# A decode step of attention and GLU layers: transposes of a kept V tile moved, one weight load halved, one sum read from PSUM

## The chip, the cores and the metric

The kernel runs on one core of one Trainium2 chip. The metric is the device time of one execution in microseconds (us). Before the change the median of three runs is 180.24 us (179.0 to 181.01).

## What is computed

Four rows of activations (batch 4, one position each, width 512) pass through attention, a gated linear unit (GLU), and then both again with the same weights and caches. There are 32 query heads on 8 key/value heads, and a window of the last 2048 positions.

```python
def _A_ref(x, k_cache, v_cache, wq, wo):
    ...
    q = (lambda x, *d: x.transpose(*d))((x @ wq).reshape(B, Sq, Hq, Dh), 0, 2, 1, 3)
    k = jnp.repeat(k_cache[:, :, Sk - W:, :], rep, axis=1)
    v = jnp.repeat(v_cache[:, :, Sk - W:, :], rep, axis=1)
    scores = jnp.einsum("bhqd,bhkd->bhqk", q, k) * (Dh ** -0.5)
    p = _softmax(scores, axis=-1)
    o = jnp.einsum("bhqk,bhkd->bhqd", p, v)
    return (lambda x, *d: x.transpose(*d))(o, 0, 2, 1, 3).reshape(B, Sq, Hq * Dh) @ wo

def _B_ref(x, w_gate, w_up, w_down):
    ...
    h = _sigmoid(g) * u
    return jnp.einsum("bsf,fd->bsd", h, w_down)

x = A_x
x = x + _A_ref(_layernorm(x, axis=-1), A_k_cache, A_v_cache, A_wq, A_wo)
x = x + _B_ref(_layernorm(x, axis=-1), B_w_gate, B_w_up, B_w_down)
x = x + _A_ref(_layernorm(x, axis=-1), A_k_cache, A_v_cache, A_wq, A_wo)
x = x + _B_ref(_layernorm(x, axis=-1), B_w_gate, B_w_up, B_w_down)
```

Both passes use the same weights and caches; `B_x` is not used.

## The kernel before

**A plan, then an order.** The Python code first records operations (`P.op`) with the tokens that they read and write and the PSUM banks that they touch. A list scheduler with assumed durations then gives each engine its order, and semaphore waits are derived from the dependencies. From the second attention on, the TensorE operations keep the order in which they were recorded (`P.chain`). An extra edge (`after=`, or `deps.add`) forces an order that the data alone do not ask for.

**Loads.** SyncE issues all weight and cache loads from line 398, in one fixed order, on one queue. SBUF is an arena of 50 slots of 512 KB (128 partitions by 4 KB). K of all eight heads stays resident for the second attention, as do the output weights `wo`. V tiles (1 MB each, one for a head `h` and a pair of batch rows `bp`) are mostly loaded again. Around the first GLU, where K and `wo` hold nearly all slots, pieces of 448 or 512 KB pass through a few half slots: `GB` (a pair), `GA` (V of head 6), and `Y` and `Z` (the two V tiles of head 7). The gate pieces go, in order, to GB0, GB1, GA0 and Y0; the up pieces to Y1, Z0, GB0 and GB1; then come the down pieces and the second attention's query weights. A load is issued as soon as the readers of its half slot are done.

**V kept in PSUM.** So that the tile `Y` and half of `Z` need not be read from HBM again, their contents are parked in PSUM banks: VectorE transposes them there in 128x512 fp32 blocks. `stash` (line 574) does four blocks of `Y`, called st0 to st3; st0 and st1 free the half Y0, st2 and st3 the half Y1. `stash_half` (line 596) does two blocks of `Z`, called so0 and so1. Later transposes bring them back (lines 589 and 602).

**The end of the first attention.** For each head, `pv_unit` multiplies V by the probabilities (line 966), VectorE normalises (`oe`, line 974), TensorE regroups the heads (`pm`, line 984) and VectorE masks the outcome (`oq`, line 989). `wo_unit` (line 1153) then multiplies by the head's output weights, accumulating in PSUM bank WB; x itself was added into the same bank at the start. After the eighth head `attn_add(0)` (line 1278) sums the four head groups in WB to the new x.

**Layer norm and GLU.** `layer_norm` sums x over its four column groups (`ln_red`, line 740), a matmul with ones gives the mean (line 743), and two subtractions (lines 746 and 750) give the centred x, as bf16 for the matmuls (`xn`) and in fp32. The GLU's gate and up products follow (line 1330, one piece of weights after the other), the gate's exponential, and the down product (line 1396). The second layer norm then feeds the query products (line 788). In the last GLU the down product runs at line 1371; its four blocks of 128 columns are copied from PSUM by ScalarE and VectorE in turn (`oc0` to `oc3`, line 1382) and one DMA writes the output.

Of the kernel before, what the change touches and what calls it, by code (L numbers as in the profile page):

```python
# [9 lines left out]
ALU = mybir.AluOpType  # L10
AXX = mybir.AxisListType.X
# [267 lines left out]
def build(nc, A_x, A_k, A_v, A_wq, A_wo, B_wg, B_wu, B_wd, out, cfg=None):  # L279
    cfg = dict(cfg or {})  # L280
    tm = dict(_TM)
# [40 lines left out]
    with es:  # L322
# [57 lines left out]
        def slot_ap(s):  # L380
            return arena[:, s * SLOT:(s + 1) * SLOT]

        def tile_ap(s):
            return arena[:, s * SLOT:(s + 2) * SLOT]
# [4 lines left out]
        def c_dve(n, rate=None):  # L389
            return tm["dve_fix"] + n * (tm["dve_f32"] if rate is None else rate)  # L390
# [147 lines left out]
        def load_wo(hh):  # L538
            left["wo", hh] = 4

            def emit(s):
                for n in range(2):
                    dma("wo%d" % (2 * hh + n), slot_ap(s + n), wo_d[:, 2 * hh + n, :], w=[("slot", s + n)], rate="bw_4k")

            if 2 * hh + 2 < HKV:
                load(("wo", hh), 4, "bw_4k", (2 * SLOT, wo_d[:, hh * 2:(hh + 1) * 2, :], False))
            else:
                loads.append((("wo", hh), emit))
# [31 lines left out]
        def named(name):  # L580
            return [o for o in P.ops if o.name == name]
# [9 lines left out]
                    o.deps.update(fresh)  # L591
            loads.append((name, emit))

        def stash_half(n, name):
            src = slot_ap(base[Z])[:, n * 1024:(n + 1) * 1024].bitcast(F32)
            P.op("vector", "so%d" % n, c_dve(512), lambda v: v.transpose(ps[:, OBS[n], :], src),
                 r=[("slot", base[Z])], w=[("so", n)], banks=(OBS[n],), after=[o for o in P.ops if o.name == name])

        def unstash_half(after):
            for n in range(2):  # L600
# [126 lines left out]
        def bview(t, b0, b1):  # L727
            return t.rearrange("p (c b) -> p c b", b=NB)[:, :, b0:b1]

        def layer_norm(tag, b0, b1, for_q):  # L730
            ds = tm["dve_small"]
            nb = b1 - b0
            xts = [("xT", b) for b in range(b0, b1)]
# [2 lines left out]
            msq = ps[:, CB, 200:200 + nb]  # L736
            ones_d = inv_d[:, 0:1].broadcast_to([128, 128])
            x2 = xT[:, NX:2 * NX]
            P.op("vector", "ln_red" + tag, ds,
                 lambda v: v.tensor_reduce(lnr[:, 0:nb], xT[:, 0:NX].rearrange("p (c b) -> p b c", c=NC), AXX, ALU.add),  # L740
                 r=xts, w=[("lnr", 0)])
            P.op("tensor", "ln_sum" + tag, tm["pe_f32"],
                 lambda t: t.matmul(mean, ones_d, lnr[:, 0:nb], start=True, stop=True),
                 r=[("lnr", 0), ("inv_d",)], w=[("cb",)], banks=(CB,))
# [399 lines left out]
        def wo_unit(tag, h, ov, k2, first, final):  # L1144
            name = ("wo", h // 2)
            s = need(name)
            o = h % 2 * REP * D

            def e_wo(pe):
                last = None  # L1150
                for r_ in range(REP):
                    for c in range(NC):
                        last = pe.matmul(ps[:, WB, c * NR:(c + 1) * NR],  # L1153
                                         tile_ap(s)[:, o + r_ * D + c * 128:o + r_ * D + (c + 1) * 128],
                                         ov[:, r_ * NR:(r_ + 1) * NR], start=(first and r_ == 0 and c == 0),
                                         stop=(final and r_ == REP - 1), skip_group_check=True)
                return last
            P.op("tensor", "WO%s_%d" % (tag, h), NC * REP * tm["pe_pair"], e_wo,
                 r=[("slot", s + h % 2)] + [("op", k2)], w=[("psw",)], banks=(WB,))
            done(name)  # L1160

        def attn_first():
            def front(h):
                k_transpose(h)
                softmax_unit("0.%d" % h, h)
                turn = lambda: turn_p(0, "0.%d" % h, h % 2, PBS[h % 2])
                return turn

            for h in range(2):
                front(h)()  # L1170
            for h in range(HKV):
                tag = "0.%d" % h
                turn = front(h + 2) if h + 2 < HKV else None
                if h == HKV - 1:
                    stash(stashed, (0, 1, 2))
                    need(Z)
                op = pv_unit(tag, h, h % 2, v_tiles[(0, h)])
                if h == HKV - 1:
                    st = stash(stashed, (3,), named("oe" + tag))
                    named("oq" + tag)[0].deps.add(st)  # L1180
                    stash_half(0, "oq" + tag)
                if turn is not None:
                    turn()
                wo_unit(tag, h, op, h % 2, False, h == HKV - 1)

        def attn_second():
            hs = list(range(HKV))[::-1]
# [99 lines left out]
                 lambda v: v.tensor_tensor(xT[:, 0:NX], xT[:, NX:2 * NX], xT[:, 0:NX], ALU.add),  # L1287
                 r=[("x2",)] + [("xT", b) for b in range(NB)], w=[("xT", b) for b in range(NB)])

        def glu(k, b0, b1, last=False):  # L1290
            nb = b1 - b0
            variance = layer_norm("G%d" % k, b0, b1, False)
            if k == 0:
                stash_half(1, "ln_redG0")
                give(base[Z])
            gub = OBS
            if k == 0:
                gub = (WB, WB)
# [60 lines left out]
            if last:  # L1359
                x_rows()  # L1360
                for (a, b) in bounds_of(k):
                    name = ("wd", a, k)
                    s = need(name)

                    def e_d(pe, a=a, b=b, s=s):
                        last_ = None
                        src = tile_ap(s)
                        for fc in range(a, b):
                            for g in range(NC):
                                o = (fc - a) * D + g * 128  # L1370
                                last_ = pe.matmul(ps[32 * g:32 * g + NB, PBS[0], 0:128], hT[:, fc * NB:(fc + 1) * NB],
                                                  src[:, o:o + 128], start=False, stop=(fc == NFC - 1),
                                                  skip_group_check=True)
                        return last_
                    P.op("tensor", "gd%d_%d" % (k, a), (b - a) * 200.0, e_d,
                         r=tok(s) + [("hT",)], w=[("orow",)], banks=(PBS[0],))
                    done(name)
                orow = ebuf[0:NB, 0:half].bitcast(BF16)
                for g in range(NC):
                    eng, f = ("scalar", "copy") if g % 2 == 0 else ("vector", "tensor_copy")  # L1380
                    P.op(eng, "oc%d" % g, c_dve(128),
                         lambda e, g=g, f=f: getattr(e, f)(orow[:, g * 128:(g + 1) * 128], ps[32 * g:32 * g + NB, PBS[0], 0:128]),
                         r=[("orow",)], w=[("oc", g), ("e", g // 2)], banks=() if g else (PBS[0],))
                dma("out", out_d, orow, w=[("out_dram",)], r=[("oc", g) for g in range(NC)], rate="bw_1k", nbytes=NB * D * 2,
                    sem=("out",))
                return
# [57 lines left out]
        fill()  # L1444
        x_in()
        q_first(layer_norm("A", 0, NB, True))
        attn_first()
        attn_add(0)
        glu(0, 0, NB)
        P.chain = True  # L1450
        q_second(layer_norm("Q", 0, NB, True))
        attn_second()
        attn_add(2)
        glu(1, 0, NB, True)
        assert not loads

        order = _schedule(P.ops, tm)
# [66 lines left out]
```

## Time and profile before

| | |
|---|---|
| median of three runs | 180.24 us (179.0 to 181.01) |
| the profiled execution | 179.2 us, its span 177.5 us |
| TensorE busy (matmuls) | 101.9 us, 57% of the span |
| VectorE busy | 104.0 us, 59% |
| ScalarE busy | 32.7 us, 18% |
| GpSimd busy | 21.6 us, 12% |
| read from HBM | 70.26 MB, 396 GB/s over the span |
| mean granted TensorE clock | 0.944 |
| first attention's last output product (line 1153) | 104.58 to 105.15 us |
| first GLU (lines 740 to 1396) | about 105.4 to 118.2 us |
| output DMA issued | 175.79 us |

Times inside the profile count from the span's start. In the rows of a timeline the first number is the start, the second the duration of the row's instructions together; then engine, line, operation, and in brackets how long the engine was idle before and which engine's event ended that. PE is TensorE, PEld its weight loads, DVE VectorE, ACT ScalarE, SPq the issuing queue of SyncE. A row of windows has the stretch, its length, the busy time of PE, PEld, DVE, ACT and POOL (with the number of instructions), the granted clock, the DMA share and GB/s. A row of the chain has start, duration and what it was.

### The profile page before, as it was taken

The page shows a single profiled execution, that of the slowest core. Times are in us where ns is not written, and L with a number is a line of the kernel's source. Part 1 is how long each engine was busy: PE and PEld are TensorE (multiplying, and loading weights), DVE is VectorE, ACT ScalarE, POOL GpSimd, SP SyncE. Part 2 cuts the span into 40 slices and gives each one's busy share as a digit, 9 for nine tenths or more (in the row PEclk, how much of TensorE's full clock was granted, in tenths as well). Part 3 has the DMA queues.
Part 4 walks back from the last instruction along what each step waited for, and adds up shares of the span by engine and source line. Part 5 has one row for each costly group of instructions (what it writes and reads, how often), then busy time and mean ns, then how long its engine had stood idle before and what let it go on. Part 6 is the DMA issues. An engine that isn't in the chain of part 4 may idle for free.

```text
span 177.5 us, 3885 instructions
## 1 busy us (share of the span) xinstructions
PE 101.9 (57%) x1641; PEld 54.8 (31%) x1653; DVE 104.0 (59%) x256; ACT 32.7 (18%) x87; POOL 21.6 (12%) x88
## 2 busy tenths in 40 slices
PE   0635326481843635607417866456886999775763
PEld 0202102241431421503404852141323444435421
DVE  7308997838476374593473492332299999742341
ACT  2002031212030300300201101000043455430011
POOL 6100010101010100100100100000011453342000
PEclk9999999999999999999999999999999999975555
DMA  5999999999999999999999999999999999999990
GB/s 191 415 430 425 423 425 415 412 423 423 419 413 418 419 428 414 414 419 423 417 423 419 410 403 378 410 406 398 382 370 414 425 425 421 415 419 401 411 372 27
DMA packets 12738, 70.52 MB, mean 397 GB/s; under 512 B 1320, under 2 KB 1328, under 8 KB 6576
## 3 DMA queue, kind: packets, MB, share of 16 engines
q1 hardware_dynamic: 12712, 70.26, 97.1%
q8 instruction: 13, 0.21, 0.5%
q14 instruction: 5, 0.04, 0.1%
q10 hardware_dynamic: 8, 0.00, 0.0%
HBM read 70.26 MB, written 0.00 MB: 396 GB/s over the span
## 4 chain that ended last, share of the span: by engine, by line
DMA 35%; DVE 33%; PE 19%; issue 4%; SPq 4%; ACT 3%; POOL 1%; DVEq 0%; ACTq 0%
DMA arena<-in_A_v_cache_dram 15%; DMA arena<-in_B_w_down_dram 13%; DVE arena L847 11%; PE ps L876 7%; DVE nmax L889 5%; DMA arena<-in_A_wq_dram 4%; PE ps L966 4%; SPq L398 4%; DMA arena<-in_B_w_gate_dram 3%; PE ps L865 2%; DVE nmax L893 2%; DVE arena L1057 2%; DVE mxt L897 2%; DVE ebuf L924 2%; PE ps L1153 2%
## 5 line engine op out<-in xcount | busy, mean ns | idle before, releaser
L847 DVE STREAM_TRANSPOSE arena<-arena 128x1024 f32<-128x1024 f32 x32 | 37.0, 1202 | 0.0
L876 PE MATMUL ps<-arena,qbd 128*32 128x512 bf16 x256 | 25.6, 535 | 0.0
L889 DVE TENSOR_REDUCE nmax<-ps 128x1 f32<-128x512 f32 x16 | 10.8, 676 | 19.5 <-PE ps L876 19.3
L865 PE MATMUL ps<-msk_m,msk_s 128*32 128x512 bf16 x64 | 8.6, 526 | 23.2 <-DVE arena L847 21.8
L966 PE MATMUL ps<-ebuf,arena 128*128 128x8 bf16 x576 | 17.6, 168 | 7.4 <-DMA arena<-in_A_v_cache_dram 4.3
L966 PEld LDWEIGHTS ps<-ebuf,arena 128*128 128x128 bf16 x576 | 16.7, 104 | 9.3 <-DMA arena<-in_A_v_cache_dram 5.3
L904 ACT ACTIVATE prow<-ps,nmax 128x512 bf16<-128x512 f32 x16 | 11.0, 687 | 35.1 <-DVE nmax L901 29.5
L840 ACT CAST qbd<-ps 128x256 bf16<-128x256 f32 x16 | 5.9, 370 | 45.0 <-PE ps L876 35.1
L933 POOL CAST s<-psm 128x1 bf16<-128x1 f32 x9 | 1.7, 187 | 83.9 <-ACT prow L904 83.9
L876 PEld LDWEIGHTS ps<-arena,qbd 128*32 128x32 bf16 x256 | 8.4, 121 | 10.3 <-issue 7.7
L788 PE MATMUL ps<-arena,xn 128*4 128x512 bf16 x64 | 8.4, 572 | 5.4 <-DMA arena<-in_A_wq_dram 5.0
L919 ACT CAST prow<-ps 128x512 bf16<-128x512 f32 x16 | 9.4, 586 | 9.9 <-PE ps L966 2.1
L1330 PE MATMUL ps<-arena,xn 128*4 128x448 bf16 x64 | 7.7, 551 | 3.7 <-DMA arena<-in_B_w_up_dram 1.9
L924 DVE STREAM_TRANSPOSE ebuf<-prow 128x256 f32<-128x256 f32 x16 | 7.0, 435 | 3.8 <-ACT prow L919 3.7
L865 PEld LDWEIGHTS ps<-msk_m,msk_s 128*32 128x32 bf16 x64 | 1.7, 98 | 24.1 <-DVE arena L847 22.7
L800 DVE STREAM_TRANSPOSE ebuf<-ps 128x512 f32<-128x512 f32 x3 | 2.1, 717 | 10.6 <-PE ps L788 10.5
L766 ACT ACTIVATE lnv<-ps 128x4 f32<-128x4 f32 x4 | 0.7, 173 | 41.2 <-PE ps L762 41.2
L1048 PE MATMUL ps<-arena,ebuf 128*32 128x512 bf16 x112 | 7.9, 404 | 0.2 <-DVE nmax L901 0.2
L835 PE MATMUL ps<-qh,eyew 32*128 32x64 bf16 x64 | 5.6, 217 | 3.7 <-ACT qbd L840 2.4
L974 DVE TENSOR_TENSOR onb<-ps,rinv 128x16 bf16<-128x16 f32 x9 | 1.6, 182 | 9.5 <-PE ps L966 9.5
L1153 PE MATMUL ps<-onp,arena 128*128 128x16 bf16 x144 | 5.3, 175 | 2.7 <-DVE onp L989 2.4
L1339 DVE STREAM_TRANSPOSE ebuf<-ps 128x448 f32<-128x448 f32 x4 | 2.6, 649 | 6.6 <-PE ps L1330 6.6
(111 smaller groups left out, 131.8 us busy)
## 6 DMA issues: line engine op xcount, KB each, us to landing
arena<-in_A_v_cache_dram SPq DMA_DIRECT2D x27, 1024.0 KB, 22.4
arena<-in_A_k_cache_dram SPq DMA_DIRECT2D x16, 1024.0 KB, 25.2
arena<-in_A_wq_dram SPq DMA_DIRECT2D x4, 1024.0 KB, 7.9
arena<-in_A_wq_dram SPq DMA_DIRECT2D x8, 512.0 KB, 6.4
arena<-in_A_wo_dram SPq DMA_DIRECT2D x3, 1024.0 KB, 26.2
arena<-in_B_w_down_dram SPq DMA_DIRECT2D x4, 512.0 KB, 6.3
arena<-in_B_w_gate_dram SPq DMA_DIRECT2D x4, 448.0 KB, 8.5
arena<-in_B_w_up_dram SPq DMA_DIRECT2D x4, 448.0 KB, 5.4
```

The lines of the kernel that those rows point to most:

```text
L788: last = pe.matmul(ps[32 * hh:32 * hh + NB, qb, :], xn[:, c * NB:(c + 1) * NB], src[:, o + hh * 512:o + (hh + 1) * 512], start=(c == 0), s ...
L847: P.op("vector", "T%d_%d" % (h, t), c_dve(1024), lambda v, v32=v32: v.transpose(v32, v32), r=[("slot", 4 * h + t)], w=[("slot", 4 * h + t)])
L865: last = pe.matmul(ps[32 * gi:32 * gi + 32, bank, :], msk_s[:, :], msk_m[:, :].unsqueeze(1).broadcast_to([128, 256, 2]), start=True, stop= ...
L876: last = pe.matmul(ps[32 * gi:32 * gi + 32, bank, :], qbd[:, q0:q0 + 32], kt[:, cp // 2, cp % 2, jh * NJ:(jh + 1) * NJ, :], start=False, s ...
L889: lambda v: v.tensor_reduce(nmax[:, k2:k2 + 1], ps[:, bank, :], AXX, ALU.max),
L904: lambda a: a.activation(prow[:, :].rearrange("p (m x t) -> p m x t", x=32, t=2), ps[:, bank, :].rearrange("p (m t x) -> p m x t", x=32, t ...
L919: P.op("scalar", "pc" + tag, c_act(512), lambda a: a.copy(prow[:, :], ps[:, pb, :]), r=[("ppb", pb)], w=[("prow",)], banks=(pb,))
L924: P.op("vector", "pt" + tag, c_dve(256), lambda v: v.transpose(et, prow[:, :].bitcast(F32)), r=[("prow",)], w=[("e", k2)])
L966: last = pe.matmul(ps[:, ob, bp * 8:bp * 8 + 8], src[:, j * 128:(j + 1) * 128], ev[:, j % 2, j % 16 // 2, x0:x0 + 8], start=(j == 0), stop ...
L1048: last = pe.matmul(ps[32 * g:32 * g + 32, ob, :], ew[:, g, mq, t], src.rearrange("p (m t d) -> p t m d", t=2, d=128)[:, t], start=(n == 0) ...
L1153: last = pe.matmul(ps[:, WB, c * NR:(c + 1) * NR], tile_ap(s)[:, o + r_ * D + c * 128:o + r_ * D + (c + 1) * 128], ov[:, r_ * NR:(r_ + 1) ...
L1330: last = pe.matmul(ps[32 * g:32 * g + NB, gub[n], 0:NF], xn[:, c * NB:(c + 1) * NB], slot_ap(s)[:, g * NF:(g + 1) * NF], start=(c == 0), s ...
```

## The change

There are four edits.

- In `attn_first` two of the four `stash` blocks (st0, st1) are recorded ahead of head 6's normalisation, the other two (st2, st3) between head 6's `oq` and head 7's normalisation; so0 stands between head 7's `oe` and `oq`, and so1 behind that `oq`, where the half slot `Z` is given back. Before, st0 to st2 followed head 6's `oq`, st3 and so0 lay around head 7's `oq`, and so1 followed the first GLU's `ln_red`.
- The last 512 KB of output weights (head 7) are loaded as two DMAs of 256 KB, and head 7's output product of the first attention is split in two, the second part waiting for the second half.
- The first GLU's `ln_red` sums the 64 columns of WB directly, and the head sum (`attn_add(0)`) is recorded behind it. `ln_red` is forced behind so1.
- The four final copies no longer write the tokens `("e", 0)` and `("e", 1)`.

In the built program TensorE has 32 of head 7's V matmuls ahead of head 6's `pm`, where it had them behind.

```diff
@@ load_wo
-                for n in range(2):
-                    dma("wo%d" % (2 * hh + n), slot_ap(s + n), wo_d[:, 2 * hh + n, :], w=[("slot", s + n)], rate="bw_4k")
+                h = 2 * hh
+                dma("wo%d" % h, slot_ap(s), wo_d[:, h, :], w=[("slot", s)], rate="bw_4k")
+                n = REP * D // 2
+                a = dma("wo%da" % (h + 1), slot_ap(s + 1)[:, 0:n], wo_d[:, h + 1, 0:n], w=[("slot", s + 1)], rate="bw_4k")
+                b = dma("wo%db" % (h + 1), slot_ap(s + 1)[:, n:2 * n], wo_d[:, h + 1, n:2 * n], w=[("half",)], rate="bw_4k")
+                b.deps.update(a.deps)
@@ layer_norm
-        def layer_norm(tag, b0, b1, for_q):
+        def layer_norm(tag, b0, b1, for_q, add=None):
...
+            part, rd, bk, after = add or (xT[:, 0:NX], xts, (), None)
             P.op("vector", "ln_red" + tag, ds,
-                 lambda v: v.tensor_reduce(lnr[:, 0:nb], xT[:, 0:NX].rearrange("p (c b) -> p b c", c=NC), AXX, ALU.add),
-                 r=xts, w=[("lnr", 0)])
+                 lambda v: v.tensor_reduce(lnr[:, 0:nb], part.rearrange("p (n b) -> p b n", b=nb), AXX, ALU.add),
+                 r=rd, w=[("lnr", 0)], banks=bk)
+            if after is not None:
+                after()
@@ wo_unit
+            half = REP // 2 if tag == "0.%d" % (HKV - 1) else REP
+            for r0 in range(0, REP, half):
+                def e_wo(pe, r0=r0):
+                    last = None
+                    for r_ in range(r0, r0 + half):
...
+                P.op("tensor", "WO%s_%d_%d" % (tag, h, r0), NC * half * tm["pe_pair"], e_wo,
+                     r=[("half",) if r0 else ("slot", s + h % 2)] + [("op", k2)], w=[("psw",)], banks=(WB,))
@@ attn_first
                 if h == HKV - 1:
-                    stash(stashed, (0, 1, 2))
+                    oe, oq = named("oe0.%d" % (h - 1)), named("oq0.%d" % (h - 1))
+                    oe[0].deps.add(stash(stashed, (0, 1)))
+                    st = stash(stashed, (2, 3), oq)
                     need(Z)
                 op = pv_unit(tag, h, h % 2, v_tiles[(0, h)])
                 if h == HKV - 1:
-                    st = stash(stashed, (3,), named("oe" + tag))
-                    named("oq" + tag)[0].deps.add(st)
-                    stash_half(0, "oq" + tag)
+                    oe, oq = named("oe" + tag), named("oq" + tag)
+                    oe[0].deps.add(st)
+                    oq[0].deps.add(stash_half(0, oe))
+                    so = stash_half(1, oq)
+                    give(base[Z])
@@ glu
-            variance = layer_norm("G%d" % k, b0, b1, False)
-            if k == 0:
-                stash_half(1, "ln_redG0")
-                give(base[Z])
+            variance = layer_norm("G%d" % k, b0, b1, False, add)
@@ glu, the final copies
-                         r=[("orow",)], w=[("oc", g), ("e", g // 2)], banks=() if g else (PBS[0],))
+                         r=[("orow",)], w=[("oc", g)], banks=() if g else (PBS[0],))
@@ build
-        attn_first()
-        attn_add(0)
-        glu(0, 0, NB)
+        so = attn_first()
+        n = len(P.ops)
+        glu(0, 0, NB, (ps[:, WB, 0:REP * NX], [("psw",)], (WB,), lambda: attn_add(0)))
+        P.ops[n].deps.add(so)
```

More of the change, by code (lines that the diff above doesn't have):

```diff
@@ L592, in load_stash, with stash_half @@
             loads.append((name, emit))
-        def stash_half(n, name):
+        def stash_half(n, after):
             src = slot_ap(base[Z])[:, n * 1024:(n + 1) * 1024].bitcast(F32)
-            P.op("vector", "so%d" % n, c_dve(512), lambda v: v.transpose(ps[:, OBS[n], :], src),
-                 r=[("slot", base[Z])], w=[("so", n)], banks=(OBS[n],), after=[o for o in P.ops if o.name == name])
+            return P.op("vector", "so%d" % n, c_dve(512), lambda v: v.transpose(ps[:, OBS[n], :], src),
+                        r=[("slot", base[Z])], w=[("so", n)], banks=(OBS[n],), after=after)
         def unstash_half(after):
@@ L1147, in wo_unit @@
             o = h % 2 * REP * D
[L1149 to L1159, printed above, removed]
+            half = REP // 2 if tag == "0.%d" % (HKV - 1) else REP
[3 more added lines that the diff above has]
+                    for r_ in range(r0, r0 + half):
+                        for c in range(NC):
+                            last = pe.matmul(ps[:, WB, c * NR:(c + 1) * NR],
+                                             tile_ap(s)[:, o + r_ * D + c * 128:o + r_ * D + (c + 1) * 128],
+                                             ov[:, r_ * NR:(r_ + 1) * NR], start=(first and r_ == 0 and c == 0),
+                                             stop=(final and r_ == REP - 1), skip_group_check=True)
+                    return last
+                P.op("tensor", "WO%s_%d_%d" % (tag, h, r0), NC * half * tm["pe_pair"], e_wo,
+                     r=[("half",) if r0 else ("slot", s + h % 2)] + [("op", k2)], w=[("psw",)], banks=(WB,))
             done(name)
@@ L1184, in attn_first @@
                 wo_unit(tag, h, op, h % 2, False, h == HKV - 1)
+            return so
         def attn_second():
@@ L1288, in attn_add, with glu @@
                  r=[("x2",)] + [("xT", b) for b in range(NB)], w=[("xT", b) for b in range(NB)])
-        def glu(k, b0, b1, last=False):
+        def glu(k, b0, b1, add=None, last=False):
             nb = b1 - b0
-            variance = layer_norm("G%d" % k, b0, b1, False)
-            if k == 0:
-                stash_half(1, "ln_redG0")
-                give(base[Z])
+            variance = layer_norm("G%d" % k, b0, b1, False, add)
             gub = OBS
@@ L1453, in build @@
         attn_add(2)
-        glu(1, 0, NB, True)
+        glu(1, 0, NB, last=True)
         assert not loads
```

## The prediction

> **What bounds the kernel now.** I read the page first, its slices and the DMA table.
>
> ```profile
> DMA  5999999999999999999999999999999999999990
> GB/s 191 415 430 425 423 425 415 412 423 423 419 413 418 419 428 414 414 419 423 417 423 419 410 403 378 410 406 398 382 370 414 425 425 421 415 419 401 411 372 27
> HBM read 70.26 MB, written 0.00 MB: 396 GB/s over the span
> ```
>
> The DMA engines are busy in every slice but the ends, and the bytes are the work: 70.26 MB at the 420 GB/s of the level slices are 167 us of the 177.5 us span. What is left is a start, a tail, and a shallow dip in slices 23 to 30 (about 102 to 133 us). The change lies in that dip, between the first attention and the first GLU. So I read next the chain of waits there, and its end:
>
> ```profile
> 100.65 0.21 DVE onb L974
> ...
> 100.90 0.28 PE ps L984 x4
> 101.18 1.58 PE ps L966 x60
> 102.76 6.09 DMA arena<-in_B_w_gate_dram
> ...
> 174.39 0.41 PE ps L1371 x8
> ...
> 174.83 0.26 ACT ebuf L1382
> ...
> 175.11 0.28 DVE ebuf L1382
> ```
>
> The chain names the load of the fourth gate piece (wg3), issued at 102.76, 6.09 us to its landing. Whether an earlier issue would land it earlier the chain can't say; the spacing of the landings can. The timeline of the TensorE:
>
> ```profile
> 107.77 0.54 PE L1330 MATMUL ps<-arena,xn 128*4 128x448 bf16 x4 [0.22 <-DMA arena<-in_B_w_gate_dram]
> ...
> 108.89 0.54 PE L1330 MATMUL ps<-arena,xn 128*4 128x448 bf16 x4 [0.58 <-DMA arena<-in_B_w_gate_dram]
> ...
> 111.13 0.54 PE L1330 MATMUL ps<-arena,xn 128*4 128x448 bf16 x4 [0.30 <-DMA arena<-in_B_w_up_dram]
> ...
> 115.91 0.50 PEld L1396 LDWEIGHTS ps<-hT,arena 128*128 128x128 bf16 x16 [0.42 <-DMA arena<-in_B_w_down_dram]
> ...
> 117.19 0.50 PEld L1396 LDWEIGHTS ps<-hT,arena 128*128 128x128 bf16 x16 [0.78 <-DMA arena<-in_B_w_down_dram]
> ...
> 117.86 0.29 PEld L1396 LDWEIGHTS ps<-hT,arena 128*128 128x128 bf16 x8 [0.17 <-DMA arena<-in_B_w_down_dram]
> ```
>
> These starts, released by landings, mark the stream's pace: wg2 to wg3 1.12 us for 448 KB (410 GB/s), wg3 to wu1 2.24 us for two more, so 1.12 each again. The last-arriving engine was never out of work here, although three of these loads were issued late. That is the reading on which the forecast stands: the issue-to-landing time on the chain is mostly queueing.
>
> **The change, part by part.** Durations are those of the profiled execution: 179.2 us, of which the span is 177.5 and 1.7 lie around it.
>
> (1) V's transposes forward. None is added: six stand on VectorE before and after (three in 1.90 us, then 0.73 each alone). The order of the built program, seen in this timeline:
>
> ```profile
> 100.65 0.20 DVE L974 TENSOR_TENSOR onb<-ps,rinv 128x16 bf16<-128x16 f32 x1 [1.44 <-PE ps L966]
> ...
> 101.21 0.23 DVE L989 TENSOR_TENSOR onp<-ps,maskp 128x64 bf16<-128x64 f32 x1 [0.37 <-PE ps L984]
> 101.36 1.90 DVE L574 STREAM_TRANSPOSE ps<-arena 128x512 f32<-128x512 f32 x3
> ...
> 105.19 0.23 DVE L1278 TENSOR_REDUCE xT<-ps 128x16 f32<-128x64 f32 x1
> 105.45 0.18 DVE L740 TENSOR_REDUCE lnr<-xT 128x4 f32<-128x16 f32 x1
> 105.67 0.73 DVE L596 STREAM_TRANSPOSE ps<-arena 128x512 f32<-128x512 f32 x1
> 105.69 0.59 PE L743 MATMUL ps<-lnr,inv_d 128*128 128x4 f32 x2 [0.53 <-DVE lnr L740]
> ```
>
> The first two (st0, st1) go ahead of head 6's normalisation (L974), which now waits for them. VectorE is idle for 1.44 us there, from 99.21; they take 2 x 0.63 = 1.27. They need the V tile of head 7, whose landing no row shows. Upper bound: 101.03, when its matmuls begin. Estimate: head 6's output weights are waited for until 103.14; back from there by 512 KB and 1 MB at 420 GB/s (1.25 + 2.5 us) gives 99.4. I take that: st1 ends at 100.65, just in time. On TensorE 32 matmuls of head 7 (0.93 us, half of 1.85) now stand ahead of head 6's regrouping (L984): it starts at 101.55 instead of 100.90, and L989 follows at 101.87. Then st2 and st3 to 103.40; head 7's L974 behind them at 103.43 (before 103.17); its regrouping to 103.98; so0 from 103.65 to 104.38, head 7's L989 to 104.63 (before 104.44). Queued behind that L989 are the last output weights' matmuls on TensorE: 0.59 us from 104.66, to 105.25 (before 105.15). So1 follows on VectorE, 104.66 to 105.39, and the mean's sum waits for it.
>
> (2) The mean from PSUM. The sum now reads 64 columns of PSUM instead of 16 of SBUF: 0.23 us by the L1278 row, 0.18 by the L740 row; I take 0.20. The head sum (0.23) leaves the chain for the cover of the ones-matmul (0.59). But so1 (0.73), which had that cover, now stands ahead. Before: L740 ends at 105.63. After: 105.42 + 0.20 = 105.62. **Gain at the mean: nothing**; the normalised x stands at 106.3 as before. If the cover were gone, the head sum's 0.23 would be back.
>
> (3) Buffers come free earlier: wg3 (by st1 and the 32 matmuls) at 101.6 instead of 102.76; the first up piece (by st3) at 103.4 instead of 104.1; the second (by so1) at 105.4 instead of 106.4. By the spacing above that is worth nothing on the slowest engine. By the windows' rates it is worth what the dips cost:
>
> ```profile
> 104.00:106.00 2.00, 0.89 (x18) 0.82 (x18) 1.79 (x6) 0.00 (x0) 0.00 (x0) 1.00 1.02 402
> 106.00:108.00 2.00, 1.42 (x14) 0.41 (x13) 0.92 (x5) 0.00 (x0) 0.00 (x0) 1.00 1.03 384
> 108.00:110.00 2.00, 1.38 (x10) 0.59 (x6) 0.51 (x1) 0.01 (x1) 0.00 (x0) 1.00 1.04 410
> 110.00:112.00 2.00, 1.09 (x8) 0.21 (x8) 1.08 (x4) 0.72 (x4) 0.00 (x0) 1.00 0.97 366
> ```
>
> Against 410 GB/s the two low windows lack 26 x 2 + 44 x 2 = 140 KB, 0.34 us. Bounds 0 and -0.34; I take -0.1, nearer the spacing, since the last landing decides.
>
> (4) The last output weights in two halves: one more DMA, 2 KB rows in place of 4 KB. SyncE's queue gets one more issue (0.33 to 0.43 us) at 96 us, ahead of wg0 and wg1, which are not needed for ten us: hidden. On the engines the nearest row is the 256 KB piece with 2 KB rows that ends the first down projection: 0.67 us behind its neighbour, where a half of 1.28 would be 0.64. Two halves: +0.06 us; bounds -0.02 (0.63 for the like piece that ends the kernel) and +0.4 if a boundary stalled one engine.
>
> The Trainium skill speaks against this split: "DMA: Bandwidth & Descriptors", section "Anatomy of one DMA", gives each DMA of the software path a fixed 2.0 us, and section "Bandwidth" advises batches of 1 MiB and over. Charged in full, the sum would be 1.9 us worse, 181.8. The 0.67 us row says that behind a filled queue the fixed part is overlapped, and the measurement decides.
>
> (5) What the words of the change leave out: the final copies (L1382) lose a write token that made the first VectorE copy wait for the first ScalarE copy. Before: ScalarE at 174.83, VectorE only at 175.11, two copies to 175.71, output issue at 175.79. After, VectorE waits for the last matmul alone and starts at 174.83 too: **-0.28 us**, at the very end, with nothing behind it to take it back. The cost if both engines disturbed each other: the copies that overlapped already took 0.26 and 0.28, so none.
>
> Sum: 0 - 0.1 + 0.06 - 0.28 = **-0.3 us**: 178.9 on the profiled 179.2. The profiled run stands 1.0 below the median of 180.24 and within its runs (179.0 to 181.01), so against the median: **179.9 us**, its own range 179.4 to 180.4.
>
> **The rivals.** A, the chain at its word: wg3's issue is 1.15 us earlier, and everything behind moves with it, since up to 133 us each load waits for a buffer that an earlier load frees. With the tail -1.4: 178.8. For it: chain and window dips; against it: the 1.12 us spacing.
>
> B, nothing comes through: the end copies are not on the path (the output's own issue and landing set the end), the dips were not issue. 180.2. Against it: the chain ends on just these copies.
>
> C, slower: st0 waits for head 7's V with head 6's L974 behind it, TensorE's regrouping behind that, and the mean behind all. If the tile lands as late as 101.0, the line shifts by 1.65 us: x at 107.95. Gate pieces 0 and 1 then free their buffers 1.65 late, and the third up load is issued at 108.9 instead of 107.2. The shortest issue to landing in this stretch is 4.7 us, so it lands at 113.6 where its matmuls began at 112.27: +1.3, less 0.28, so 181.3. It decides from about 0.3 us of delay of x on, as that load had 5.0 us. For it: there is no slack in step 1; against it: the landing worked out at 99.4.
>
> **How the numbers follow.** Forecast 0.55, A 0.12, B 0.13, C 0.20. The range 178.7 to 181.3 takes in A's and C's times and leaves out some 0.15 for the scatter of medians about them. One per cent is 1.8 us, about what a measurement of this kernel can tell from no change; the forecast and B lie well inside. Faster by more needs A with more dips filled: 0.07. Slower by more needs C in full and lost pace as well: 0.08. Within: 0.85.
>
> **What would show it.** Right: transposes ahead of 100.65; x at 106.3 +/- 0.2; wg3 issued near 101.6 yet its matmuls still 1.1 us behind wg2's; both engines' final copies starting together. Wrong: gate and up matmuls earlier by 0.5 or more (A), x later than 106.6 with the up pieces waited for longer (C), or the last down pieces landing over 0.5 us off 173.7 with the GLU unchanged, a cause that I have not named.

## The result, and the profile after

| | before, same group | after | ratio after/before, 95% interval |
|---|---|---|---|
| first group, 22 runs each | 179.73 us (178.65 to 181.01) | 178.77 us (178.46 to 179.66) | 0.9953 [0.9931, 0.9975] |
| second group, 12 runs after | 179.63 us | 179.25 us | 0.9999 [0.9964, 1.0034] |
| third group, 12 runs after | 179.94 us | 179.38 us | 0.9986 [0.9947, 1.0025] |

The ratios are of the fast runs of each side, so they are not the quotients of the medians beside them. The second and third rows are the same changed kernel, run again as a measure for the experiments (e5_again, e11_third). Weighted by the inverse squares of their half widths (0.0022, 0.0035, 0.0039) the three ratios give 0.9970, plus or minus 0.0017: about -0.5 us. But the three lie somewhat further apart than these widths explain: none of the first group's 22 runs of the changed kernel is above 179.66 us, while 4 and 5 of the 12 in the repeats are above 180. Widened for that (a factor of 1.7), the interval is plus or minus 0.0028, that is 0 to -1.0 us. The change makes the kernel a little faster, by less than 1%; the first group alone shows that clearly, the two repeats do not.

The profiled execution after took 178.55 us with a span of 176.8 (before 179.2 and 177.5). Its page, slices and bytes:

```profile
DMA  5999999999999999999999999999999999999991
GB/s 183 426 428 424 423 423 417 411 426 419 417 413 421 423 419 421 411 424 424 411 417 432 400 402 392 406 405 382 410 398 406 423 423 419 419 417 407 405 388 39
HBM read 70.26 MB, written 0.00 MB: 397 GB/s over the span
```

The bytes are the same. Slices 23 to 26 (97 to 115 us) after the change read 400, 402, 392, 406 where before they read 410, 403, 378, 410: the stretch that the change edits moves as much as before. Slices 28 to 30 (119 to 133 us), where both programs are the same, read 382, 410, 398 in place of 398, 382, 370, in sum 40 more.

VectorE in the timeline after (start, duration, engine, line, operation, idle time and what ended it):

```profile
98.95 0.26 DVE L957 RECIPROCAL rinv<-ps 128x16 f32<-128x16 f32 x1
99.30 1.32 DVE L578 STREAM_TRANSPOSE ps<-arena 128x512 f32<-128x512 f32 x2
100.73 0.20 DVE L981 TENSOR_TENSOR onb<-ps,rinv 128x16 bf16<-128x16 f32 x1
...
101.87 0.23 DVE L996 TENSOR_TENSOR onp<-ps,maskp 128x64 bf16<-128x64 f32 x1 [0.95 <-PE ps L991]
102.13 1.32 DVE L578 STREAM_TRANSPOSE ps<-arena 128x512 f32<-128x512 f32 x2
...
103.55 0.19 DVE L981 TENSOR_TENSOR onb<-ps,rinv 128x16 bf16<-128x16 f32 x1
103.78 0.73 DVE L600 STREAM_TRANSPOSE ps<-arena 128x512 f32<-128x512 f32 x1
...
104.61 0.23 DVE L996 TENSOR_TENSOR onp<-ps,maskp 128x64 bf16<-128x64 f32 x1
104.87 0.73 DVE L600 STREAM_TRANSPOSE ps<-arena 128x512 f32<-128x512 f32 x1
104.98 0.58 PE L1162 MATMUL ps<-onp,arena 128*128 128x16 bf16 x16 [0.90 <-DVE onp L996]
105.70 0.23 DVE L745 TENSOR_REDUCE lnr<-ps 128x4 f32<-128x64 f32 x1
105.84 0.21 DVE L1292 TENSOR_REDUCE xT<-ps 128x16 f32<-128x64 f32 x1
105.98 0.59 PE L750 MATMUL ps<-lnr,inv_d 128*128 128x4 f32 x2 [0.42 <-DVE lnr L745]
106.60 0.17 DVE L753 TENSOR_TENSOR xn<-xT,ps 128x16 bf16<-128x16 f32 x1 [0.55 <-PE ps L750]
```

The line numbers have moved: L578 and L600 are the two kinds of transposes (L574, L596 before), L981, L991 and L996 the normalisation, regrouping and mask of a head, L745 and L750 the mean, L753 the centred x (`xn`). The two early transposes begin at 99.30. VectorE was free from 99.21, and by the trace the last share of the tile `Y` (V of head 7) landed at 99.28, so they start right behind that landing. The head sum (L1292) now stands behind the sum for the mean (L745), which reads PSUM. x is ready at 106.60; before it was 106.31.

The pieces of weights on TensorE, after:

```profile
106.92 1.41 PE L1341 MATMUL ps<-arena,xn 128*4 128x448 bf16 x12 [0.36 <-DVE xT L757]
108.92 0.54 PE L1341 MATMUL ps<-arena,xn 128*4 128x448 bf16 x4 [0.58 <-DMA arena<-in_B_w_gate_dram]
...
111.14 0.54 PE L1341 MATMUL ps<-arena,xn 128*4 128x448 bf16 x4 [0.28 <-DMA arena<-in_B_w_up_dram]
...
115.93 0.50 PEld L1407 LDWEIGHTS ps<-hT,arena 128*128 128x128 bf16 x16 [0.44 <-DMA arena<-in_B_w_down_dram]
...
117.22 0.50 PEld L1407 LDWEIGHTS ps<-hT,arena 128*128 128x128 bf16 x16 [0.79 <-DMA arena<-in_B_w_down_dram]
...
117.90 0.29 PEld L1407 LDWEIGHTS ps<-hT,arena 128*128 128x128 bf16 x8 [0.17 <-DMA arena<-in_B_w_down_dram]
```

108.92, 111.14, 115.93, 117.22, 117.90 after; 108.89, 111.13, 115.91, 117.19, 117.86 before. SyncE issued the fourth gate piece at 101.75 instead of 102.76 and the two first up pieces at 103.47 and 105.67 instead of 104.13 and 106.42, and none of them landed earlier. The third and fourth up pieces were issued 0.29 us later than before (107.51 and 107.88 for 107.22 and 107.59), since x came later, and did not land later: 112.21 and 113.33, before 112.22 and 113.32.

The end of the kernel after:

```profile
174.03 0.10 PEld L1382 LDWEIGHTS ps<-arena,hT 128*4 128x4 bf16 x8 [0.32 <-DMA arena<-in_B_w_down_dram]
174.47 0.54 ACT L1393 CAST ebuf<-ps 4x128 bf16<-4x128 f32 x2 [5.38 <-PE ps L1382]
174.47 0.61 DVE L1393 CAST ebuf<-ps 4x128 bf16<-4x128 f32 x2 [2.94 <-PE ps L1382]
175.15 0.35 SPq L398 DMA_DIRECT2D out_dram<-ebuf  x1
```

Both engines copy from 174.47. From the last matmuls' weights (174.03) to the output's issue (175.15) is 1.12 us; before it was 1.40 (174.39 to 175.79).

So of the 0.7 us between the two spans (0.64 unrounded), 0.28 is at the very end, nothing is there at 118 us, and the other 0.4 comes up behind 119 us, where the change edits nothing. By the last landings it is not there yet at 128 us (the last query load landed at 128.41 after, 128.40 before); it is 0.22 us at 138 (138.28, 138.50) and 0.36 at the last load (173.99, 174.35). What that 0.4 is, and whether it belongs to the change, is the question of the experiments.

### The profile page after: what moved, and what is told of

Its sections match the earlier page's. It is cut to its first block, busy times and chain, and to the rows that moved or that the text cites. A ratio compares the mean times of both kernels' runs of the same rounds, so it can differ in the third digit from the quotient of the medians.

```text
span 176.8 us, 3904 instructions
## 1 busy us (share of the span) xinstructions
PE 105.5 (60%) x1653; PEld 54.7 (31%) x1653; DVE 104.2 (59%) x256; ACT 32.7 (18%) x87; POOL 21.6 (12%) x88
## 4 chain that ended last, share of the span: by engine, by line
DMA 38%; DVE 32%; PE 19%; SPq 4%; issue 3%; ACT 2%; DVEq 0%; ACTq 0%
DMA arena<-in_B_w_down_dram 15%; DMA arena<-in_A_v_cache_dram 15%; DVE arena L854 11%; PE ps L883 7%; DVE nmax L896 5%; DMA arena<-in_B_w_gate_dram 4%; DMA arena<-in_A_wq_dram 4%; SPq L398 4%; PE ps L973 3%; PE ps L872 2%; DVE nmax L900 2%; DVE mxt L904 2%; DVE ebuf L931 2%; PE ps L924 2%; DVE arena L1064 2%
## 5 line engine op out<-in xcount | busy, mean ns | idle before, releaser
L883 PE MATMUL ps<-arena,qbd 128*32 128x512 bf16 x256 | 25.0, 525 | 0.1
L924 PE MATMUL ps<-prow,perm 128*128 128x512 bf16 x16 | 7.9, 496 | 8.2 <-ACT prow L911 8.2
L1055 PE MATMUL ps<-arena,ebuf 128*32 128x512 bf16 x112 | 7.3, 381 | 0.2 <-DVE nmax L908 0.2
L981 DVE TENSOR_TENSOR onb<-ps,rinv 128x16 bf16<-128x16 f32 x9 | 1.7, 185 | 8.3 <-PE ps L973 8.1
```

The source lines that it names most:

```text
L883: last = pe.matmul(ps[32 * gi:32 * gi + 32, bank, :], qbd[:, q0:q0 + 32], kt[:, cp // 2, cp % 2, jh * NJ:(jh + 1) * NJ, :], start=False, s ...
L924: lambda pe: pe.matmul(ps[:, pb, :], perm[:, :], prow[:, :], start=True, stop=True),
L1055: last = pe.matmul(ps[32 * g:32 * g + 32, ob, :], ew[:, g, mq, t], src.rearrange("p (m t d) -> p t m d", t=2, d=128)[:, t], start=(n == 0) ...
```

## Experiments: the parts of the change

Two theories stand against each other. The first: besides the copies, the earlier issue of three loads is worth the rest. The second: the rest is not the change's, but differs from execution to execution.

**The copies alone** (e1_copies, on the kernel before), and **everything but the copies** (e2_no_copies, on the kernel after, the line the other way):

```diff
-                         r=[("orow",)], w=[("oc", g), ("e", g // 2)], banks=() if g else (PBS[0],))
+                         r=[("orow",)], w=[("oc", g)], banks=() if g else (PBS[0],))
```

> The kernel before with one edit: the four final copies lose the extra write token, so VectorE's first copy waits only for the last matmul. Theory 1 (the sum of the prediction): -0.28 us on the span's end, ratio 0.9984, and nothing before 174 us changes. Theory 2 (the copies are all of the gain, and the load stream contributes by chance only): the whole -0.84 us, ratio 0.9953. Theory 3 (the output's own issue and landing set the end): ratio 1.000.

> The changed kernel with the write token of the final copies put back; all else as changed. Theory 1 (copies -0.28, the rest from the load stream between 118 and 134 us): ratio to the kernel before 0.997, -0.56 us. Theory 2 (copies are all): 1.000. The final copies start one after the other again, 0.28 us apart.

The ends of the two timelines, the copies alone first:

```profile
176.17 0.10 PEld L1371 LDWEIGHTS ps<-arena,hT 128*4 128x4 bf16 x8 [0.32 <-DMA arena<-in_B_w_down_dram]
176.61 0.54 ACT L1382 CAST ebuf<-ps 4x128 bf16<-4x128 f32 x2 [6.45 <-PE ps L1371]
176.61 0.61 DVE L1382 CAST ebuf<-ps 4x128 bf16<-4x128 f32 x2 [2.89 <-PE ps L1371]
177.29 0.34 SPq L398 DMA_DIRECT2D out_dram<-ebuf  x1
```

```profile
174.56 0.10 PEld L1382 LDWEIGHTS ps<-arena,hT 128*4 128x4 bf16 x8 [0.32 <-DMA arena<-in_B_w_down_dram]
174.99 0.54 ACT L1393 CAST ebuf<-ps 4x128 bf16<-4x128 f32 x2 [5.83 <-PE ps L1382]
175.28 0.61 DVE L1393 CAST ebuf<-ps 4x128 bf16<-4x128 f32 x2 [3.19 <-ACT ebuf L1393]
175.96 0.35 SPq L398 DMA_DIRECT2D out_dram<-ebuf  x1
```

With the edit the tail takes 1.12 us (176.17 to 177.29), without it 1.40 (174.56 to 175.96). That is the -0.28 us of the prediction, the same to 0.01 us in every profile of either kind. As a time it can't be resolved: 179.53 us, ratio 0.9996 [0.9949, 1.0043], and 179.45 us, 0.9988 [0.9945, 1.0032]. The profile of the copies alone even has the longer span, 179.0 us. Its loss lies far ahead of the tail. Windows from 124 to 132 us (columns as before; the last is GB/s): the kernel before, the copies alone, the kernel after:

```profile
124.00:128.00 4.00, 3.32 (x32) 1.11 (x32) 0.98 (x2) 0.37 (x1) 0.00 (x0) 1.00 1.02 390
128.00:132.00 4.00, 3.60 (x40) 1.15 (x37) 3.49 (x9) 1.90 (x5) 0.00 (x0) 1.00 1.02 359
```

```profile
124.00:128.00 4.00, 3.32 (x32) 1.15 (x36) 0.98 (x2) 0.37 (x1) 0.00 (x0) 1.00 0.97 341
128.00:132.00 4.00, 3.11 (x44) 1.03 (x37) 2.92 (x8) 1.33 (x4) 0.00 (x0) 1.00 0.89 329
```

```profile
124.00:128.00 4.00, 3.58 (x32) 1.04 (x32) 0.76 (x2) 0.37 (x1) 0.00 (x0) 1.00 1.03 413
128.00:132.00 4.00, 2.97 (x41) 0.98 (x37) 3.62 (x9) 2.01 (x5) 0.07 (x1) 1.00 1.05 399
```

All three do the same work here; the counts differ only by where its edges fall. 390 and 359 against 341 and 329 GB/s is 316 KB in 8 us, between the kernel before and the copies alone, two programs that differ only in a wait nearly 50 us later. So this stretch differs between executions by more than the whole effect that is looked for.

**The output weights whole again** (e3_whole_wo, on the kernel after: one load of 512 KB, one output product), and **the split alone** (e6_split_only, on the kernel before):

```diff
-            half = REP // 2 if tag == "0.%d" % (HKV - 1) else REP
+            half = REP
```

> The changed kernel with the last output weights in one load and one block of matmuls again. Theory A (the earlier release of the buffers brings the stream's part, the split costs 0.06 us): ratio 0.995 to the kernel before, as the change or slightly better. Theory B (the split brings the stream's part, because it shifts which engine is behind): ratio 0.998, the copies alone.

> The kernel before with the last output weights in two loads and two blocks of matmuls, nothing else. By the prediction's sum +0.06 us, ratio 1.000. A rival that the first group leaves open (kernels with the split were quicker by 0.5 us than those without, copies set aside): ratio 0.997.

Without the split 180.02 us, 1.0001 [0.9961, 1.0042]; the split alone 180.62 us, 1.0038 [1.0005, 1.0072]. The one run says that the split helps, the other that it harms. Neither is told apart from the scatter between groups (the unchanged program's three ratios lie from 0.9953 to 0.9999), so its price stays open between the two; nothing here speaks for the +0.4 that a stalled engine would have cost at once, since the loads behind it land at the old times (the first gate piece at 105.50 after, 105.51 before).

**The old order of the transposes** (e4_old_stash, on the kernel after; the mean from PSUM, the copies and the split stay):

```diff
-                    oe, oq = named("oe0.%d" % (h - 1)), named("oq0.%d" % (h - 1))
-                    oe[0].deps.add(stash(stashed, (0, 1)))
-                    st = stash(stashed, (2, 3), oq)
+                    stash(stashed, (0, 1, 2))
...
+            if k == 0:
+                stash_half(1, named("ln_redG0"))
+                give(base[Z])
```

> The changed kernel with the transposes of V in their old places, and the last one behind the mean's sum, which is still read from PSUM; copies and split as changed. The mean is then earlier by 0.25 us (x near 106.1), and the up load into Z is issued behind the last transpose, near 106.2. Theory A (earlier release brings the stream's part): ratio 0.998, the copies alone, wg3 issued near 102.7 again. Theory B (the split brings it) or an earlier mean that feeds the third and fourth up load sooner: ratio 0.995 or better.

179.07 us, 0.9977 [0.9937, 1.0018]: in the middle of the three ratios of the whole change. Its timeline takes the mean apart:

```profile
105.10 0.23 DVE L745 TENSOR_REDUCE lnr<-ps 128x4 f32<-128x64 f32 x1
105.37 0.72 DVE L600 STREAM_TRANSPOSE ps<-arena 128x512 f32<-128x512 f32 x1
...
106.01 0.17 DVE L753 TENSOR_TENSOR xn<-xT,ps 128x16 bf16<-128x16 f32 x1
106.12 1.60 SPq L398 DMA_DIRECT2D arena<-in_B_w_up_dram  x3
...
111.19 0.54 PE L1339 MATMUL ps<-arena,xn 128*4 128x448 bf16 x4 [0.29 <-DMA arena<-in_B_w_up_dram]
```

With the sum from PSUM and so1 behind it, x is ready at 106.01: 0.30 earlier than before (106.31). Moving the transposes forward costs that and as much again (106.60). Neither shows in a load: the second up piece's matmuls start at 111.19 here, at 111.14 in the whole change and at 111.13 before.

## Experiments: is the issue of the loads worth anything?

If an earlier issue gains, a later one must lose. In **e7_hold_up1** the second up load waits for the first gate matmuls, in **e10_hold_less** only for the mean's ones-matmul. Both stand on the kernel after:

```diff
+        byname = dict((o.name, o) for o in P.ops)
+        byname["('wu', 1, 0)"].deps.add(byname["glwg0_0"])    # e10: "ln_sumG0"
```

> The changed kernel with the second up load held back until the first gate piece's matmuls are done, about 107.5 instead of 105.7 us. Theory A (late issue starves the DMA engines that are ahead, the lead that they had is gone, and a later fetch of program code on any of them then delays the whole stream): its matmuls still start near 111.2, but the median is 0.3 to 0.6 us above the changed kernel's, ratio 0.998 to 1.001. Theory B (only the landing of the slowest engine counts, and that moves by under 0.1 us): ratio as the changed kernel's in this group.

> The changed kernel with the second up load held until the mean's ones-matmul is done, so that it is issued at about 106.5 us, where the kernel before issued it (106.42), instead of 105.67. Theory of the lead (a late issue takes from the engines that are ahead the lead that later hides a code fetch): 0.3 to 0.8 us above the changed kernel in the same group, 179.4 to 180.0, ratio to the kernel before 0.998 to 1.003; the second up piece's matmuls still begin near 111.1. Rival, the issue has slack until the slowest engine runs dry: as the changed kernel within 0.2 us, ratio 0.995 to 0.998.

> The changed kernel itself once more, beside the others of this group. Theory 1 (the end copies are -0.28 us and the stream gains as well): ratio near 0.995 again. Theory 2 (the first comparison had chance on its side; copies and nothing else): ratio 0.998. In every profile the out DMA is issued 1.12 us behind the start of the last eight matmuls, 1.40 in the kernel before.

> The changed kernel itself once more, as the measure for the other two runs of this group. Both theories: 178.7 to 179.3 us, ratio to the kernel before 0.994 to 0.999.

The held load in e7's timeline, and TensorE behind it:

```profile
107.43 1.28 SPq L398 DMA_DIRECT2D arena<-in_B_w_up_dram  x3
...
111.02 0.54 PE L1341 MATMUL ps<-arena,xn 128*4 128x448 bf16 x4 [0.23 <-DMA arena<-in_B_w_up_dram]
112.14 0.54 PE L1341 MATMUL ps<-arena,xn 128*4 128x448 bf16 x4 [0.58 <-DMA arena<-in_B_w_up_dram]
...
113.98 0.54 PE L1341 MATMUL ps<-arena,xn 128*4 128x448 bf16 x4 [1.29 <-DMA arena<-in_B_w_up_dram]
```

Held by 1.76 us (107.43 for 105.67), the load lands no later: its matmuls start at 111.02 (111.14 without the hold). The loss appears two loads on, at 113.98 (113.37 without), and the end is later still: 181.11 us, 1.0093 [1.0063, 1.0122], beside 0.9999 for the unchanged program in the same group. In e10 the load is issued at 106.78, 0.36 us later than in the kernel before; 180.58 us, 1.0031 [0.9996, 1.0066], beside 0.9986 [0.9947, 1.0025]. By the two ratios that is 0.8 us more, the upper end of what the theory of the lead gave; but their intervals overlap, so for e10 alone this is not settled.

Why a load can be late at its issue and not at its landing is seen when the 16 DMA engines are kept apart. A load is done when its last engine is done; the trace has the end of each engine's share:

| | second up load issued | it lands: first engine | last engine | fourth up load lands: first | last |
|---|---|---|---|---|---|
| after | 105.67 | 109.23 | 111.09 | 111.53 | 113.33 |
| e4 (old order) | 106.12 | 109.23 | 111.15 | 111.47 | 113.40 |
| before | 106.42 | 109.30 | 111.09 | 111.80 | 113.32 |
| e7 | 107.43 | 110.08 | 110.97 | 112.55 | 113.94 |

In these loads the engines run 0.9 to 1.9 us apart. The late issue in e7 starves the engines that are ahead (109.23 becomes 110.08) and not the last one (111.09, 110.97). It takes their lead. Between 105.67 and 106.42, the range in which the change moves this issue, even the first engine hardly notices, and the last landing is the same to 0.1 us. So the earlier issue that the change brings can be worth little; that is shown as far as the landings go, and e4's time (0.9977) agrees with it. Why e7's fourth up load then lands 0.6 us late is not shown: it was issued at 108.28, 5.7 us before its landing, while the second needed only 3.5 (107.43 to 110.97), so its own issue does not look too late.

## Experiments: the code that is fetched

What differs from execution to execution in the stretch behind 118 us? Besides the loads, the DMA engines serve one more queue. The page after has it so, and the page before has the same line:

```profile
q8 instruction: 13, 0.21, 0.5%
```

Thirteen packets of 16 KB of program code; by the trace after, each takes 1.02 to 1.11 us, on one engine at a time. One of them starts between 118.5 and 120.9 us in each of the profiles below. The query weights land there one after another, 1.28 us apart (512 KB each), and behind this fetch the last landing falls back by an amount that is not the same twice:

| kernel (profiled execution) | late against the 1.28 us spacing, this load and the next | span |
|---|---|---|
| e4 | 0.04 | 176.8 |
| after | 0.11 | 176.8 |
| after again (e5) | 0.41 | 177.1 |
| before | 0.42 | 177.5 |
| e2 | 0.42 | 177.6 |
| e3 | 0.24 | 178.2 |
| e12 (below) | 0.37 | 179.0 |
| after again (e11) | 0.63 | 178.9 |
| e7 | 0.77 | 179.3 |
| e1 | 1.16 | 179.0 |
| e6 | 1.17 | 179.5 |
| e9 (below) | 1.28 | 179.6 |

The loss is between nothing and about the length of the fetch, and three executions of one program have 0.11, 0.41 and 0.63. That the fetch makes the loss when it falls on an engine that is already last, and none when its engine is ahead, fits these numbers; which engine is hit was not forced in a run, so it is argued and not shown. The longest spans have the largest losses, but the span grows by more than this one loss (e3 and e12 lose little here and more elsewhere), and where the rest is added was not taken apart. Nor is this row the 0.4 us between the profiles before and after: the kernel before loses 0.31 more here, but the kernel after loses 0.27 further on (125.88 behind 124.33, for 1.28), and the last query load lands at the same time in both. So the source of that 0.4 stays open. The same changed program has spans of 176.8, 177.1 and 178.9, so the 0.4 isn't shown to belong to the change.

**More code** (e8_more_code, on the kernel after: 96 small matmuls behind the output product of five heads, 960 TensorE instructions):

```diff
+                if h < HKV - 3:
+                    ...
+                    P.op("tensor", "more%d" % h, 96 * tm["pe_pair"], e_more,
+                         r=[("permo",)] + perms, w=[("psw",)], banks=(WB,))
```

> The changed kernel with 96 more small matmuls (into unused columns, never read) behind each of the output products of heads 0 to 4, where TensorE waits for VectorE: 960 more instructions, so some 4 more fetches of 16 KB of program code by the DMA engines, before 80 us. Theory F (each fetch holds one DMA engine for 1.0 to 1.1 us, and the end is set by the engine with most of them): 17 fetches instead of 13 in the profile, the stream's last landings about 0.3 us later at the median, with single executions in steps of about 1 us. Rival (fetches are hidden): ratio as the changed kernel's. If the added matmuls delay the scores, the V tiles' issue would show it.

182.56 us, 1.0161 [1.0123, 1.0198]. The page has three packets of code more:

```profile
q8 instruction: 16, 0.26, 0.6%
```

TensorE stands still three times (1.10, 1.04 and 0.98 us) with nothing to wait for that the profile shows; one of the three rows:

```profile
104.83 0.43 PE L973 MATMUL ps<-ebuf,arena 128*128 128x8 bf16 x10 [0.98 <-issue]
```

The three stops end at 46.39, 68.35 and 104.83, which is 2.56, 2.56 and 2.48 us after the start of a code fetch (43.83, 65.79 and 102.35). The one stop in e9, below, ends 2.57 us after one (104.05 and 101.48). The other twelve profiles, from 12 us on, have no stop of this kind of 0.3 us or more. So four of four stops follow a fetch by the same time, as they would if TensorE waited for that code.

So the loss isn't the fetches' DMA time alone: the work itself and these stops make the units late too (the second up load was issued at 107.41). The run shows that code has a price here, not how it divides.

**Less code** (e9_one_mask, on the kernel after; four mask matmuls of 32 columns become one of 128), and the same **with its code put back in place** by 24 small matmuls (e12_one_mask_pad):

```diff
-                for gi in range(4):
-                    last = pe.matmul(ps[32 * gi:32 * gi + 32, bank, :], msk_s[:, :],
-                                     msk_m[:, :].unsqueeze(1).broadcast_to([128, 256, 2]), start=True, stop=False)
+                return pe.matmul(ps[:, bank, :], msk4[:, :],
+                                 msk_m[:, :].unsqueeze(1).broadcast_to([128, 256, 2]), start=True, stop=False)
```

> The changed kernel with the four 32-column mask matmuls that open each score unit written as one 128-column matmul (the same sums in PSUM; 96 TensorE instructions fewer, and some 0.35 us less of TensorE in each unit). Theory of the fetches (each block of program code that is fetched holds one DMA engine for 1.05 us, and the last lander pays when it is the engine hit): 96 instructions are some 0.4 of a block, so 12 or 13 fetches stand in the profile in place of 13, and their places shift; 0 to -0.5 us against the changed kernel itself in the same group (178.6 to 179.2), ratio to the kernel before 0.993 to 0.997. Rival, bytes alone set the end: no difference from the changed kernel in the group, within 0.2 us. Third, TensorE's units matter: queries and gate matmuls would start some 0.3 us earlier; not expected, since loads release them.

> The kernel with one mask matmul for each score unit, and 24 small matmuls (48 TensorE instructions, read by nobody) behind the first head's output weights in the first attention, where TensorE waits for loads. The merged masks save 48 instructions up to the end of the first attention, so these put TensorE's code near 100 us back to the place that it has in the changed kernel. The kernel without them lost its time where TensorE stood still for 1.45 us at 102.6 behind a code fetch at 101.5. Theory that the place of the code makes the loss: the fetch is back at about 98.8, the stop is gone, the second up load is issued near 105.7 again, and the time is 178.6 to 179.4 us, ratio to the kernel before 0.993 to 1.000. Rival, the merged matmul itself costs the time (a longer unit, other waits): 180.9 to 181.8, ratio 1.006 to 1.012. Third, the place matters and falls badly in another way: the stop is elsewhere in the stretch from 95 to 136 us, 180 to 181.5.

Meant as a gain, e9 is slower: 181.37 us, 1.0101 [1.0064, 1.0138], with 12 packets of code for 13. Its timeline has two reasons. The first, on TensorE, directly behind a code fetch at 101.48:

```profile
104.05 0.64 PE L975 MATMUL ps<-ebuf,arena 128*128 128x8 bf16 x18 [1.45 <-issue]
```

A stop of 1.45 us in the middle of a head's V matmuls. With the code back in place the same stretch runs through:

```profile
102.39 0.99 PE L975 MATMUL ps<-ebuf,arena 128*128 128x8 bf16 x32
```

e12 takes 180.62 us, 1.0053 [1.0015, 1.0091]: 0.0048 less than e9, but the two intervals overlap, so what the stop costs in time is not settled. The second reason is the merged matmul itself, which was expected to save. The mask and the scores behind it, in the kernel after and then in e12:

```profile
92.33 0.62 PE L872 MATMUL ps<-msk_m,msk_s 128*32 128x512 bf16 x4 [4.40 <-DVE arena L854]
92.73 1.50 PE L883 MATMUL ps<-arena,qbd 128*32 128x512 bf16 x12
```

```profile
92.86 0.61 PE L875 MATMUL ps<-msk_m,msk 128*128 128x512 bf16 x1 [4.40 <-DVE arena L859]
93.40 1.04 PE L885 MATMUL ps<-arena,qbd 128*32 128x512 bf16 x8
```

Four narrow matmuls take as long as one wide one (0.62 and 0.61), and the scores may start behind them after 0.40 us, where the wide one holds them for 0.54. The delay grows with every unit: in e12 the mask of this unit and of the four before it starts 0.07, 0.19, 0.30, 0.42 and 0.53 us late, and in e9 it is the same to 0.01. The gate and up loads are then issued up to 0.7 us late (the third up load at 108.22, after 107.51; in e9 at 108.69). So e12's theory and its rival both held in part: with the code back in place the stop is gone, and the merged matmul delays the units on its own. Its theory's time (178.6 to 179.4) did not come.

No kernel here beats the changed one: the best other ratio, e4's 0.9977, lies within its three.

## Why the prediction was right, and where not

The forecast was 0.3 us faster and within 1%, and a small gain within 1% is what came: 0.9970 over three groups. That the range held is in part luck: the first group's 178.77 lies 0.07 above its lower end (178.7), and by the medians the first group's gain is 0.96 us, three times the forecast. Only the 0.28 of the copies is shown as such. By the steps of the prediction:

- **What bounds the kernel.** Right. Issues up to 1.0 us earlier left the landings where they were (108.92 for 108.89, 117.90 for 117.86), as the spacing of landings had said and the chain had not. The table of engines agrees with "the last-arriving engine was never out of work": the last share lands at the same time whether the issue is at 105.67 or 106.42. (The dip of slices "23 to 30, about 102 to 133 us" begins at 97.6 us by the width of a slice; nothing rests on it.)
- **(1) Transposes.** The tile `Y` of head 7 landed at 99.28 (estimated 99.4), and the regrouping started at 101.58 (forecast 101.55). Behind that small sums went the wrong way: so1 began at 104.87, not 104.66, since head 7's normalisation, so0 and its mask ahead of it were late by 0.12, 0.13 and 0.21.
- **(2) The mean.** "Gain at the mean: nothing" was off: x came at 106.60 and not at 106.3 +/- 0.2. The reduction from PSUM took 0.23 (0.20 taken) and began 0.10 behind so1's end (0.03 taken); with so1's 0.21 that makes the 0.3. e4 shows the two sides of the sum: the new source is worth 0.30, the moved transposes cost 0.59. It cost no time, because the fourth gate piece's landing, not x, released the matmuls at 108.92.
- **(3) Earlier issue, -0.1 us.** Neither confirmed nor refuted. What is left of the measured -0.54 (0.0030 of 179.8) behind the copies' -0.28 is -0.26, with 0.5 on either side. e4, with the old issue times, loses nothing. What the prediction did not see is the other side: the second up load issued 1.0 us later than before, and the two behind it 0.6 to 0.7, cost 0.9% (e7). So an issue 1.0 us later than in the kernel before is too late; at 0.36 us (e10) it is not settled.
- **(4) The split, +0.06 us.** No run resolves it; no load behind it landed later. The whole fixed part that the prediction weighed (1.9 us) is excluded: e6's interval ends at 1.0072, 1.3 us, and the second half landed at 104.38, where the whole load landed at 104.36 before. (That figure is for the software path; the profile's queue table lists these loads as `hardware_dynamic`.)
- **(5) The copies, -0.28 us.** Right to 0.01 us in the rows, in each profile with and without the edit; the times can't resolve it.
- **The number itself.** 179.9 us was 1.13 above the 178.77 of the first group, and outside the forecast's own 179.4 to 180.4. What was off is "against the median": the three runs' 180.24 stood 0.51 above the 179.73 that 22 runs of the same kernel gave. The other 0.62 is the first group's difference of 0.96 against the 0.34 of the sum, and the two repeats take most of that back. The 178.9 that the sum gave on the profiled run comes nearer by chance: that run (179.2) lies 0.5 below the median of 22.
- **Rival A** (the chain at its word, 178.8) has the time and not the mechanism: its sign, gate and up matmuls earlier by 0.5, is absent. **B** falls with the tail's 0.28 in the rows, not by the times. **C** falls at its condition: V did not land at 101.0, and x, although 0.29 late, made no up piece wait. Its 4.7 us from issue to landing is no floor either: e7's second up load took 3.5.

## What to carry over

Where a queue of loads is kept full, read the landings, not the issues: here three loads were issued up to 1 us earlier, and one 1.8 us later, and each landed at the same time to 0.1 us; the later issue cost 0.9% all the same, and the loss showed two loads on. A wait at the very end of the kernel, with nothing behind it, can be read from the rows (0.28 us here) even where the times can't resolve it. Base a forecast on many runs: with a scatter of 2 us between executions of one program, the median of three stood 0.51 us off that of 22, about as much as the change was worth.

## What the runs showed of the hardware that was not expected

- The 16 engines that share a load end 0.9 to 1.9 us apart in the up loads (after: 109.23 to 111.09).
- A fetch of 16 KB of program code takes 1.02 to 1.11 us on one DMA engine, 13 times in this kernel; behind the one near 119 us the stream fell back by 0.04 to 1.28 us from one execution to another. The Trainium skill, "Runtime: NRT & Kernel Launch", section "Instruction fetch mechanics", calls the cost of crossing into the next block of code "mostly hidden". The profile after counts 3306 TensorE matmuls and weight loads, 12.9 blocks of the 256 instructions that the page gives, for 13 packets. In twelve of the fourteen profiles TensorE shows no stop for it; in e9 and e8 it does, with stops of 1.45 us and of 0.98 to 1.10 us.
- Taking instructions out can bring a stop: with 96 fewer (e9) TensorE stood still for 1.45 us behind a fetch, and with 48 put back (e12) it did not.
- Four 32-column matmuls took no longer than one of 128 columns (0.62 and 0.61 us), and let what follows start 0.14 us sooner.
